# A spectral block with a SwiGLU layer in split fp32r: the first half's layout, layer two's weight parts and output sets, the order of two late steps, and where the planner's sweep begins

## The chip, the cores and the metric

The kernel runs on one core of a Trainium2 chip. The metric is the device time of one execution in microseconds, and the number for a version is the median over several runs. The core has five instruction streams that run side by side and wait for each other through semaphores: TensorE (PE in the profile) multiplies, VectorE (DVE), ScalarE (ACT) and GpSimd (POOL) do elementwise work, SyncE (SP) issues DMAs; ACT and POOL issue some too. Each stream runs its instructions strictly in order.

## The reference

A sequence of 4096 rows with 640 features goes through two residual blocks. Cut to what matters:

```python
x = A_x                                             # (1, 1, 4096, 640)
h = layernorm(x) * (1 + ca) + sa
x = x + ga * A_ref(h)
h = layernorm(x) * (1 + cb) + sb
x = x + gb * ((silu(h @ w_gate) * (h @ w_up)) @ w_down)      # w_gate: 640 x 1728

def A_ref(x):
    z = rfft2(x, axes=(1, 2)).reshape(..., 4, 160)           # H is 1: a DFT over 4096 rows
    hr = relu(zr @ w1[0] - zi @ w1[1] + b1[0])               # per block of 160
    hi = relu(zi @ w1[0] + zr @ w1[1] + b1[1])
    or_ = softshrink(hr @ w2[0] - hi @ w2[1] + b2[0], 0.01)
    oi_ = softshrink(hi @ w2[0] + hr @ w2[1] + b2[1], 0.01)
    return irfft2(or_ + 1j * oi_)
```

The six vectors sa, ca, ga, sb, cb, gb come from `silu(c) @ w_mod`. All data is float32.

## The kernel before, in words

**Split matmuls.** A float32 product is made of three fp32r products. An operand is split into a high part (a copy rounded to fp32r, mostly by ACT) and a low part (the operand minus its high part, mostly by DVE), and PE adds high·high, high·low and low·high in PSUM. So almost everything that PE multiplies has first been through ACT and then DVE, and a late low part is what PE can be seen to wait for.

**First half (to about 310 us), ordered by hand.** The rows come in as tiles `xa0` to `xa7`, are normalised, go through the first DFT step (`dft_a`) and are written to DRAM (`s1`, by `write_s1`) to be read back in another order. Then a loop over p goes through 28 regular slots (p = 0 to LAST; a slot is one block b of 160 features of one chunk ch of frequencies, p = 4 ch + b; there are 8 chunks), and a few tail slots follow. In a slot each engine gets its pieces in the order in which the calls stand:

- `stage_b(ch, t)` is the second DFT step on PE. `evac_b` splits its result into `z` (high on ACT, low on DVE: L603, L604). `evac_rh` and `evac_rl` do the same for the rest features, into `rz` (L626, L636).
- `stage_l1` is layer one (PE L657, L670). Its relu and split make `h` (ACT L660, L661, then DVE L662) and `u` (DVE L675). `tail_l1` and `tail_low` split the rest into `r` (ACT L682, DVE L687).
- `stage_l2(ch, b)` is layer two: for each half q eight matmuls into a PSUM tile `pc` (PE L707), with the weight parts `w2a`, `w2b` and `w2c`; then a DVE addition (L709) writes `pc` plus the bias into the output set `tt` of the chunk. Of a chunk's four blocks the first takes two `tt` tiles (one for each q), of which there are two in all.
- At the next chunk's first block `move_x` moves the finished set by DMA into `xx` tiles. `shrink`, `shrink_high` (ACT, `xh`) and `shrink_low` (DVE L749, `xl`) make the softshrink and its split; `stage_i` is the inverse DFT's first step (PE L760 to L762).

The weights of layer two are split by six jobs (`prep2`): for each of w2a, w2b, w2c two halves of 160 columns, o = 0 and 1. Job 0 is half 0 of w2a, job 1 half 1 of w2a, jobs 2 and 3 those of w2b, 4 and 5 those of w2c. A high part is one instruction (POOL L281 or ACT L283), a low part one on DVE (L286), except that of job 5, which POOL makes with a TENSOR_TENSOR (L523). Before the loop POOL makes the high parts of jobs 0, 2 and 5 and the low part of 5, ACT the high part of job 1, DVE the low parts of 0 and 1. In slot 0, after `stage_l2` has been called for nothing, ACT makes the high parts of 3 and 4 and DVE the low parts of 2, 3 and 4. The first layer-two matmuls stand in slot 1.

The tiles `w2a` to `w2c`, `acc`, `cl`, `wx`, `bx`, `tt` and `xx` are in a pool `p2`, opened once the pool `xp` of the `xa` tiles is closed. Its tiles take over `xp`'s memory, and an instruction that writes a tile there waits for whatever still reads the `xa` tile that had the place, among it the DMAs that write it to `s1`.

**Second half (from about 310 us), ordered by a planner.** A second layer norm and the SwiGLU layer go over six row tiles, the first two in the plain way (`plain`, PE L1951 to L1953), the last four with seven products in place of eight (`seven`, PE L2028 to L2030 and L2039 to L2041). Steps with a planned duration stand in chains: `prep` splits the weights (`wb`: ACT L1413, DVE L1420), `gate` and the others load, add up and split what the coming stages need, and `tails` holds short chains that the matmul stages leave behind: the splitting of activations (`a`, `a13`: ACT L1987, L1925, DVE L1988, L1926) and of the left operands `L` (ACT L2104, DVE L2108). While the planner walks along PE's matmuls it calls `sweep()` every 0.3 planned us; a sweep goes through the chains in a fixed order and issues (`tries`) each next step whose planned start is near enough. What comes first in a sweep takes the engine first.

Of the kernel before, what the change touches and what calls it, by code (L numbers as in the profile page):

```python
# [6 lines left out]
F32 = mybir.dt.float32  # L7
# [11 lines left out]
NB = 4  # L19
# [154 lines left out]
def body(tc, x, w1, b1, w2, b2, wg, wu, wd, c, wm, k_fa, k_tb, k_tx, k_bm, k_bx, k_ga, k_ge, k_id, out, dbg=None):  # L174
# [4 lines left out]
    def f32(ap):  # L179
        return ap.bitcast(F32)  # L180
# [21 lines left out]
    with ExitStack() as top:  # L202
# [35 lines left out]
        with ExitStack() as af:  # L238
# [101 lines left out]
            with tc.tile_pool(name="sp", bufs=1) as sp:  # L340
                xas = []

                def load_x(t):
                    xa = xp.tile([P, 4, D], F32, name=f"xa{t}")
                    if t < 3:
                        for i in range(4):
                            nc.sync.dma_start(xa[:, i, :], xv[:, 4 * t + i, :])
                    else:
                        nc.sync.dma_start(xa, xv[:, 4 * t:4 * t + 4, :])
                    xas.append(xa)  # L350
# [158 lines left out]

            acc = p2.tile([P, D], F32, name="acc")  # L510
# [3 lines left out]
            w2a = p2.tile([P, NB, 640], F32R, name="w2a")  # L514
            w2b = p2.tile([P, NB, 640], F32R, name="w2b")
            w2c = p2.tile([P, NB, 640], F32R, name="w2c")
# [3 lines left out]
            for n in (0, 2, 5):  # L520
                weights_high(*prep2[n], pool)
            w, h, l, v, _ = prep2[5]
            pool.tensor_tensor(w[:, :, l], v, f32(w[:, :, h]), op=OP.subtract)  # L523
# [61 lines left out]
            tts = {}  # L585
# [105 lines left out]
            def stage_l2(ch, b, then=()):  # L691
                h0, h1, r2, _ = hss[ch, b]
                de = slice(160 * b, 160 * b + 160)
                for q in ((0, 2, 1) if ch == CE else (0, 1)):
# [3 lines left out]
                    if b == 0 and q < 2:  # L698
                        tts[ch, q] = p2.tile([P, 2, D], F32, tag="tt", bufs=2, name=f"tt{ch}_{q}")
# [8 lines left out]
                    if q < 2:  # L708
                        dve.tensor_tensor(tts[ch, q][:, :, de], pc[:, :320].rearrange("p (r e) -> p r e", r=2),  # L709
                                          b2t[:, :, b, :], op=OP.add)  # L710
                        if then:
                            then[q]()
                    else:

                        dve.tensor_tensor(tts[ch, 0][0:1, 1, de], pc[0:1, :160], b2t[0:1, 0, b, :], op=OP.add)
# [55 lines left out]
            pool.memset(zero, 0.0)  # L771
            pool.tensor_copy(edge, zero)

# [19 lines left out]
            for job in prep2[0:2]:  # L793
                weights_low(*job)
# [31 lines left out]
            for p in range(LAST + 1):  # L826
# [22 lines left out]
                on(tail_l1, p)  # L849
                on(shrink_high, p - 6)  # L850
                for k in rows:
                    on(evac_rl, k)
                on(tail_low, p)
                on(stage_l2, p - 1)
                if p == 3:
                    stage_b(1, 2)
                    evac_b(1, 2)
                on(stage_i, p - 7)
                on(shrink_low, p - 6)
                if p < LAST:  # L860
                    on(shrink_parts, p - 5)
# [3 lines left out]
                if p == 0:  # L865
                    for n in (3, 4):
                        weights_high(*prep2[n])
                    for job in prep2[2:5]:
                        weights_low(*job)
                if p == 0:  # L870
                    pool.dma_start(bm.rearrange("p a b c -> p (a b c)"), k_bm)
# [173 lines left out]
        with ExitStack() as ff:  # L1045
# [166 lines left out]
            def sweep():  # L1212
                held = NT
                for c in tails + chains:
                    if c in tile_of:
                        if tile_of[c] > held:
                            continue
                        tries(c)
                        if c.steps:
                            held = tile_of[c]  # L1220
                    else:
                        tries(c)
                tails[:] = [c for c in tails if c.steps]
# [1293 lines left out]
```

## Time and profile before

| | us |
|---|---|
| three runs | 1419.41, 1421.2, 1422.27 (median 1421.2) |
| the profiled execution, its own time | 1421.44 |
| its span, first to last instruction | 1419.6 |
| PE busy | 1386.4 (98% of the span) |
| DVE, ACT, POOL busy | 1055.8 (74%), 766.7 (54%), 599.3 (42%) |

Where PE is busy for nearly the whole span, a shorter time can only come from the stretches in which it isn't, or from those in which its clock is lowered. The list of PE's waits names for each matmul line what ended its idle time, and the timeline shows single instructions with the idle time before them in brackets.

### The profile page before, as it was taken

To read this page: it belongs to the slowest core of one execution; us is meant where nothing else is said; L and a number is where in the kernel's file an instruction comes from. 1 tells how busy PE (TensorE), PEld (TensorE's weight loads), DVE (VectorE), ACT (ScalarE), POOL (GpSimd) and SP (SyncE) were. 2 spreads that over 40 slices of the span, in tenths; PEclk is the share of its full clock that TensorE was granted. 3 is DMA by queue.
4 is the path that set the end of the run, shared out by engine and by line. 5 is a ranking of instruction groups with operands and counts; after the bars stand their busy time and mean duration, and the time that the engine had idled before them with its cause. 6 is when DMAs were issued, how large, how long until landed. Compare 5 with 4: busy or idle time off the path is not lost.

```text
span 1419.6 us, 23748 instructions
## 1 busy us (share of the span) xinstructions
PE 1386.4 (98%) x8410; PEld 1311.5 (92%) x8410; DVE 1055.8 (74%) x1863; ACT 766.7 (54%) x1542; POOL 599.3 (42%) x681
## 2 busy tenths in 40 slices
PE   6899999999999999999999999999999999999998
PEld 2599999977989899899999999999999999999998
DVE  8979888889888888649786758787678757365654
ACT  6869999756555545546463446446264624252341
POOL 5600210047767765336454535357153524052241
PEclk9999999999999999999999999999999999999999
DMA  9866556666797997899867998788998667965634
GB/s 360 314 235 201 166 170 193 204 224 205 272 369 283 316 339 267 284 372 320 308 207 274 351 342 287 279 296 270 373 319 289 228 219 274 339 209 194 216 118 148
DMA packets 170872, 377.34 MB, mean 266 GB/s; under 512 B 22177, under 2 KB 81633, under 8 KB 168738
## 3 DMA queue, kind: packets, MB, share of 16 engines
q1 hardware_dynamic: 161650, 359.28, 72.9%
q0 software_dynamic: 6800, 13.93, 3.0%
q10 hardware_dynamic: 2304, 2.62, 0.5%
q8 instruction: 66, 1.08, 0.3%
q14 instruction: 52, 0.43, 0.1%
HBM read 269.48 MB, written 96.80 MB: 258 GB/s over the span
## 4 chain that ended last, share of the span: by engine, by line
PE 83%; DVE 5%; ACT 3%; DMA 3%; POOL 2%; issue 2%; SPq 1%; ACTq 0%; DVEq 0%; POOLq 0%
PE pw L2028 9%; PE pw L2030 9%; PE pw L2029 9%; PE pc L2329 8%; PE pd L2245 7%; PE pe L2329 6%; PE pg L1953 4%; PE pg L1952 4%; PE pg L1951 4%; PE pc L707 4%; PE pl L657 3%; PE pw L2041 2%; PE pw L2039 2%; PE pw L2040 2%; PE py L1666 2%
## 5 line engine op out<-in xcount | busy, mean ns | idle before, releaser
L1420 DVE TENSOR_TENSOR wb<-r,wb 128x768 fp32r<-128x768 f32 (+3 forms) x170 | 161.8, 961 | 11.5 <-ACT wb L1413 11.0
L2028 PE MATMUL pw<-h,wt 128*128 128x384 f32 x412 | 139.4, 338 | 1.7 <-ACT s_v L2047 1.4
L2030 PE MATMUL pw<-h,wt 128*128 128x384 f32 x412 | 138.3, 336 | 0.0
L2029 PE MATMUL pw<-h,wt 128*128 128x384 f32 x412 | 138.0, 335 | 0.0
L2108 DVE TENSOR_TENSOR L<-sg,L 128x384 fp32r<-128x384 f32 x144 | 106.8, 762 | 38.0 <-ACT L L2104 37.3
L1413 ACT ACTIVATE wb<-r 128x768 fp32r<-128x768 f32 (+3 forms) x168 | 104.3, 638 | 53.4 <-PE pw L2041 42.7
L2329 PE MATMUL pc<-wq,L 128*128 128x320 f32 x846 | 132.2, 309 | 0.0
L2329 PEld LDWEIGHTS pc<-wq,L 128*128 128x128 f32 x846 | 126.2, 188 | 0.7 <-DVE s_v L2054 0.3
L2088 POOL TENSOR_TENSOR sg<-s_x,sg 128x384 f32<-128x384 f32 x24 | 31.4, 1307 | 218.3 <-DVE s_x L2054 218.3
L2028 PE MATMUL pw<-h,wb 128*128 128x384 f32 x312 | 105.0, 336 | 0.0
L2029 PE MATMUL pw<-h,wb 128*128 128x384 f32 x312 | 104.4, 335 | 0.0
L2030 PE MATMUL pw<-h,wb 128*128 128x384 f32 x312 | 104.3, 334 | 0.0
L2329 PE MATMUL pe<-wq,L 128*128 128x320 f32 x648 | 102.4, 310 | 1.4 <-DMA wq<-wqd 1.4
L1953 PE MATMUL pg<-ht,wb 128*128 128x512 f32 x260 | 101.4, 390 | 1.5 <-DVE wb L1420 1.5
L1951 PE MATMUL pg<-ht,wb 128*128 128x512 f32 x260 | 101.9, 392 | 0.0
L2047 ACT ACTIVATE s_x<-pw 128x384 f32<-128x384 f32 x52 | 25.5, 491 | 140.9 <-PE pw L2030 138.9
L1952 PE MATMUL pg<-ht,wb 128*128 128x512 f32 x260 | 101.3, 390 | 0.0
L2099 POOL TENSOR_TENSOR sg<-sg,sg 128x384 f32<-128x384 f32 x72 | 92.1, 1279 | 17.2 <-DVE L L2108 13.7
L2329 PEld LDWEIGHTS pe<-wq,L 128*128 128x128 f32 x648 | 96.6, 188 | 1.7 <-DVE x L2286 1.7
L2245 PE MATMUL pd<-wq,a 128*128 128x320 f32 x632 | 96.0, 310 | 0.0
L2245 PEld LDWEIGHTS pd<-wq,a 128*128 128x128 f32 x632 | 93.4, 188 | 0.5
L764 POOL DMA_DIRECT2D s<-co x28 | 15.8, 563 | 180.0 <-ACT co L763 176.7
(317 smaller groups left out, 3903.3 us busy)
## 6 DMA issues: line engine op xcount, KB each, us to landing
wq<-wqd SPq DMA_DIRECT2D x83, 640.0 KB, 5.7
wt<-td SPq DMA_DIRECT2D x103, 512.0 KB, 5.2
hs<-ho SPq DMA_DIRECT2D x52, 512.0 KB, 5.9
h<-hs SPq DMA_DIRECT2D x32, 768.0 KB, 7.9
td<-wt SPq DMA_DIRECT2D x25, 512.0 KB, 5.3
r<-in_B_w_gate_dram SPq DMA_DIRECT2D x24, 384.0 KB, 5.2
r<-in_B_w_up_dram SPq DMA_DIRECT2D x24, 384.0 KB, 4.0
xx<-tt SPq DMA_DIRECT2D x56, 160.0 KB, 3.2
```

The lines of the kernel that those rows point to most:

```text
L1413: def high(ks, e=slice(0, c), copy=lambda o, i: act.activation(o, i, AF.Copy)):
L1420: dve.tensor_tensor(wbs[t, n][:, 1, ks, e], raw[t, n][:, ks, e], f32(wbs[t, n][:, 0, ks, e]), op=OP.subtract)
L1951: mm(b, wh, hh, start=(kk == 0), stop=False)
L1952: mm(b, wh, hl, start=False, stop=False)
L1953: mm(b, wl, hh, start=False, stop=(kk == 4))
L2028: mm(b, w(0, kp), a[:, kp, 0], start=start and kp == 0, stop=False, skip_group_check=not start)
L2029: mm(b, w(0, kp), a[:, kp, 1], start=False, stop=False, skip_group_check=not start)
L2030: mm(b, w(1, kp), a[:, kp, 0], start=False, stop=kp == 1, skip_group_check=not start)
L2099: pool.tensor_tensor(o, x, y, op=op)
L2108: dve.tensor_tensor(o[:, 1], raws[j], f32(o[:, 0]), op=OP.subtract)
L2245: mm(b[:, :320], l, m, start=start and i == 0, stop=stop and i == len(s) - 1)
L2329: mm(o[:, :320], ls[q][:, x, k], w[:, q, y], start=start and q == 0 and n == 0, stop=q == 1 and n == 2, skip_group_check=not start)
```

## The change

The first half, the diff cut to its core:

```diff
                 xas = []
+                xts = {t: xp.tile([P, 4, D], F32, name=f"xa{t}") for t in (1, 2, 3, 0, 4, 5, 6, 7)}
 
                 def load_x(t):
-                    xa = xp.tile([P, 4, D], F32, name=f"xa{t}")
+                    xa = xts[t]
...
+            w2a = p2.tile([P, NB, 640], F32R, name="w2a")
+            w2b = p2.tile([P, NB, 640], F32R, name="w2b")
+            w2c = p2.tile([P, NB, 640], F32R, name="w2c")
             acc = p2.tile([P, D], F32, name="acc")
             cl = p2.tile([P, D], F32, name="cl")
             wx = p2.tile([P, P], F32, name="wx")
             bx = p2.tile([P, 2, 128], F32, name="bx")
-            w2a = p2.tile([P, NB, 640], F32R, name="w2a")
-            w2b = p2.tile([P, NB, 640], F32R, name="w2b")
-            w2c = p2.tile([P, NB, 640], F32R, name="w2c")
+            p2.tile([P, 896], F32, name="gap")
+            tts = {(1, q): p2.tile([P, 2, D], F32, tag="tu", bufs=2, name=f"tt1_{q}") for q in range(2)}
             prep2 = prep_weights(raws[2], w2a, w2b, w2c, False)
 
             prep2 = [prep2[i] for i in (0, 3, 1, 4, 2, 5)]
-            for n in (0, 2, 5):
+            for n in (0, 2):
                 weights_high(*prep2[n], pool)
-            w, h, l, v, _ = prep2[5]
-            pool.tensor_tensor(w[:, :, l], v, f32(w[:, :, h]), op=OP.subtract)
+
+            def weights_rest(n):
+                w, h, l, v, _ = prep2[n]
+                pool.tensor_tensor(w[:, :, l], v, f32(w[:, :, h]), op=OP.subtract)
...
-            def stage_l2(ch, b, then=()):
+            def stage_l2(ch, b, then=(), held=None):
...
-                    if b == 0 and q < 2:
-                        tts[ch, q] = p2.tile([P, 2, D], F32, tag="tt", bufs=2, name=f"tt{ch}_{q}")
+                    if b == 0 and q < 2 and ch != 1:
+                        tts[ch, q] = p2.tile([P, 2, D], F32, tag="tu" if ch % 2 else "tt", bufs=2, name=f"tt{ch}_{q}")
...
-                        dve.tensor_tensor(tts[ch, q][:, :, de], pc[:, :320].rearrange("p (r e) -> p r e", r=2),
-                                          b2t[:, :, b, :], op=OP.add)
+                        add = lambda q=q, pc=pc: dve.tensor_tensor(
+                            tts[ch, q][:, :, de], pc[:, :320].rearrange("p (r e) -> p r e", r=2), b2t[:, :, b, :], op=OP.add)
+                        if held is None:
+                            add()
+                        else:
+                            held.append(add)
...
             weights_high(*prep2[1])
-            for job in prep2[0:2]:
-                weights_low(*job)
+            weights_low(*prep2[0])
+            weights_rest(1)
+            weights_high(*prep2[3], pool)
+            weights_rest(3)
...
-                on(tail_l1, p)
-                on(shrink_high, p - 6)
+                for f in (shrink_high, tail_l1) if p == LAST else (tail_l1, shrink_high):
+                    on(f, p if f == tail_l1 else p - 6)
                 for k in rows:
                     on(evac_rl, k)
-                on(tail_low, p)
-                on(stage_l2, p - 1)
+                if p == LAST:
+                    on(shrink_low, p - 6)
                 if p == 3:
+                    adds = []
+                    stage_l2(0, 2, held=adds)
                     stage_b(1, 2)
                     evac_b(1, 2)
+                    on(tail_low, p)
+                    for f in adds:
+                        f()
+                else:
+                    on(tail_low, p)
+                    on(stage_l2, p - 1)
                 on(stage_i, p - 7)
-                on(shrink_low, p - 6)
                 if p < LAST:
+                    on(shrink_low, p - 6)
                     on(shrink_parts, p - 5)
...
                 if p == 0:
-                    for n in (3, 4):
+                    for n in (4, 5):
                         weights_high(*prep2[n])
-                    for job in prep2[2:5]:
-                        weights_low(*job)
-                if p == 0:
+                    weights_rest(5)
+                    for n in (2, 4):
+                        weights_low(*prep2[n])
+                    pool.memset(zero, 0.0)
+                    pool.tensor_copy(edge, zero)
                     pool.dma_start(bm.rearrange("p a b c -> p (a b c)"), k_bm)
```

The second half:

```diff
             def sweep():
                 held = NT
-                for c in tails + chains:
+                for c in [gate, prep] + tails + chains:
```

What it does, part by part. (a) **Layout:** the `xa` tiles get their places in the order 1, 2, 3, 0, 4 to 7, and the weight tiles come first in `p2`. Before, `w2a`, `w2b`, `w2c` and `tt` had the places of `xa1`, `xa2`, `xa3` and `xa4`; now `w2a` lies in memory that no `xa` tile had, `w2b` on `xa1`, `w2c` on `xa2`, `acc` to `bx` on `xa3`, the new set `tu` on `xa0`, and `tt` still on `xa4`. (b) **Weight parts:** POOL makes the high parts of jobs 0, 2 and 3 and the low parts of 1, 3 and 5, ACT the high parts of 1, 4 and 5, DVE the low parts of 0, 2 and 4 only. (c) **Output sets:** chunks with an odd number write to a second set, `tu`. (d) **Slot 3:** the two additions of `stage_l2(0, 2)` are held back until `evac_b(1, 2)` and `tail_low` are issued. (e) **Slot LAST:** ACT makes `xh` ahead of the rest's relu, and DVE makes `xl` ahead of `tail_low` and of layer two's additions. (f) **Sweep:** `gate` and `prep` are tried ahead of `tails`, and again in their old place.

How the instructions moved is shown at three places. The first is POOL's stream in the first half, from layer two's first weight part on (`rm` and `rr` are the raw weights; L281 makes high parts; `bm` is the inverse DFT's matrix). Before:

```order
L281 TENSOR_SCALAR w2a<-rm_596 128x4x160
L281 TENSOR_SCALAR w2b<-rm_596 128x4x160
L281 TENSOR_SCALAR w2c<-rr_597 128x4x160
L523 TENSOR_TENSOR w2c<-rr_597,w2c 128x4x160
L771 MEMSET zero 128x40
L772 CAST edge<-zero 128x40
L871 DMA bm<-in_k_bm_dram 128x512
```

and now:

```order
L281 TENSOR_SCALAR w2a<-rm_596 128x4x160
L281 TENSOR_SCALAR w2b<-rm_596 128x4x160
L528 TENSOR_TENSOR w2a<-rm_596,w2a 128x4x160
L281 TENSOR_SCALAR w2b<-rm_596 128x4x160
L528 TENSOR_TENSOR w2b<-rm_596,w2b 128x4x160
L528 TENSOR_TENSOR w2c<-rr_597,w2c 128x4x160
L886 MEMSET zero 128x40
L887 CAST edge<-zero 128x40
L888 DMA bm<-in_k_bm_dram 128x512
```

POOL has two subtractions more, and `zero`, `edge` and the load of `bm` come behind them.

The second is DVE's stream in row tile 1, about 483 us into the span, where `wb1_3` is the weight group 3 of that tile, `wq` and `tq` are parts of the down weights, `a1_1_1_1` and `a13_1` low parts of activations, `x9` a residual row. Before:

```order
L1420 TENSOR_TENSOR wb1_3_5794<-r1_3_5388,wb1_3_5794 128x512
L1532 TENSOR_TENSOR wq1_1_1_5801<-wdr1_1_5683,wq1_1_1_5801 128x2x320
L1988 TENSOR_TENSOR a1_1_1_1_5788<-sg1_0_1_5724,a1_1_1_0_5787 128x512
L1920 TENSOR_TENSOR sgr1_5822<-pg1_2_0_5790,sgr1_5822 64x512
L1420 TENSOR_TENSOR wb1_3_5794<-r1_3_5388,wb1_3_5794 128x768
L1573 TENSOR_TENSOR tq0_1_5818<-wdr1_0_5345,tq0_1_5818 128x2x320
L1926 TENSOR_TENSOR a13_1_5821<-sgr1_5822,a13_1_5821 64x512
```

and now:

```order
L1437 TENSOR_TENSOR wb1_3_5801<-r1_3_5397,wb1_3_5801 128x512
L2005 TENSOR_TENSOR a1_1_0_1_5766<-sg1_0_0_5700,a1_1_0_0_5765 128x512
L1687 TENSOR_TENSOR x9_5577<-x9_5577,py9_0_5815 128x320
L1437 TENSOR_TENSOR wb1_3_5801<-r1_3_5397,wb1_3_5801 128x768
L2005 TENSOR_TENSOR a1_1_1_1_5795<-sg1_0_1_5727,a1_1_1_0_5794 128x512
L1937 TENSOR_TENSOR sgr1_5839<-pg1_2_0_5797,sgr1_5839 64x512
L1549 TENSOR_TENSOR wq1_1_1_5804<-wdr1_1_5698,wq1_1_1_5804 128x2x320
```

The second low part of the weight group stood behind three other instructions since the first, and now stands behind two with fewer elements; `wq`, the second `a` part and `sgr` come after it.

The third is ACT's stream at the start of row tile 2's weight group 3, about 643 us into the span (`s2_3_x`, `s2_3_v`, `s2_3_y` copy PSUM results, `a13_2_1` is an activation's high part, `ho3` the next tile's rows). Before:

```order
L2047 ACTIVATE s2_3_x_7507<-pw2_3_0_7496 128x384
L2104 ACTIVATE L05_7165<-sg2_0_10_7279 128x384
L1925 ACTIVATE a13_2_1_7492<-sgr2_1_7493 64x384
L2104 ACTIVATE L06_7166<-sg2_0_00_7274 128x384
L1766 ACTIVATE ho3_0_1_7533<-h32_3_0_7315 128x2x128 x2
L2047 ACTIVATE s2_3_v_7539<-pw2_3_3_7528 128x384
```

and now:

```order
L2064 ACTIVATE s2_3_x_7503<-pw2_3_0_7492 128x384
L1430 ACTIVATE wb2_4_7500<-r2_4_7349 128x768
L2121 ACTIVATE L05_7179<-sg2_0_10_7257 128x384
L2121 ACTIVATE L06_7180<-sg2_0_00_7252 128x384
L2064 ACTIVATE s2_3_v_7548<-pw2_3_3_7537 128x384
L1783 ACTIVATE ho3_0_0_7553<-h32_3_0_7389 128x2x128 x2
```

`s2_3_v` now stands ahead of `ho3` and of `a13_2_1`, and the weight group's larger high part ahead of `L05`.

More of the change, by code (lines that the diff above doesn't have):

```diff
@@ L584, in body @@
             hss = {}
-            tts = {}
             def width(ch):
@@ L770, in body @@
             zero = hp.tile([P, 2, 5, 2, 2], F32, name="zero")
-            pool.memset(zero, 0.0)
-            pool.tensor_copy(edge, zero)
             def edges():
```

## The prediction

> **What bounds the kernel now.** I read the page first, then the list of PE's waits, then windows, then the timeline around each long wait.
>
> ```profile
> span 1419.6 us, 23748 instructions
> PE 1386.4 (98%) x8410; PEld 1311.5 (92%) x8410; DVE 1055.8 (74%) x1863; ACT 766.7 (54%) x1542; POOL 599.3 (42%) x681
> ```
>
> PE is the bound: it idles 1419.6 − 1386.4 = 33.2 us in all, and no matmul is added or removed here. So a gain can come only from those 33.2 us and from stretches of lowered clock. The waits, by what ended them (total, times, longest):
>
> ```profile
> PE pa L437 <- ACT xa L416: 9.8, 2, 8.0
> PE pc L707 <- DVE w2b L286: 2.4, 1, 2.4
> PE py L1666 <- DVE chl L1656: 1.9, 1, 1.9
> PE pg L1953 <- DVE wb L1420: 1.5, 1, 1.5
> PE pb L596 <- DVE z L604: 1.5, 2, 1.0
> PE pi L761 <- DVE xl L749: 1.0, 1, 1.0
> PE pi L760 <- DVE u L675: 1.0, 2, 0.8
> ```
>
> The largest, 9.8, is the start, before anything that the change moves. The `chl` wait stays too: it lies between the halves, ahead of the place (about 410 us) from which the second half's order differs. What remains is a handful of waits of 1 to 2.4 us. I go through them by the parts of the change.
>
> **Slot 3, additions held back (d).**
>
> ```profile
> 88.24 0.89 DVE L709 TENSOR_TENSOR tt<-pc,b2t 128x320 f32<-128x320 f32 x2
> 89.05 0.74 DVE L604 SCALAR_TENSOR_TENSOR z<-pb,ca,z 128x512 fp32r<-128x512 f32 x1
> 89.85 1.16 PE L596 MATMUL pb<-tb,g 128*128 128x128 f32 x8 [1.03 <-DVE z L604]
> 90.76 0.69 PE L707 MATMUL pc<-w2a,h 128*128 128x320 f32 x3
> ```
>
> PE waits 1.03 us for the PSUM bank that this `z` frees, and `z` stands behind the two additions (0.89) and the `r` before them. With the additions held back `z` starts about 1.2 us earlier, ahead of the `r` too, and `stage_b` follows the matmul before it. The additions come about 0.75 later (`z`'s 0.74); they free PSUM tiles that the next layer-two group takes only from 90.76, after the end of the delayed additions at about 89.9, so they are covered. Were that cover gone, PE would lose up to 0.75. **−1.0.**
>
> **Slot LAST (e).**
>
> ```profile
> 265.95 0.72 ACT L744 ACTIVATE xh<-xx 128x640 fp32r<-128x640 f32 x1
> 267.12 0.89 DVE L709 TENSOR_TENSOR tt<-pc,b2t 128x320 f32<-128x320 f32 x2
> 267.92 0.81 DVE L749 TENSOR_TENSOR xl<-xx,xh 128x640 fp32r<-128x640 f32 x1
> 268.79 0.41 PE L761 MATMUL pi<-xl,bm 128*128 128x320 f32 x1 [1.05 <-DVE xl L749]
> ```
>
> `xl` needs only `xh`, finished at 266.67, or 266.3 with `xh` ahead of the relu. Ahead of `r` and the additions it runs at 266.7 instead of 267.9, 1.2 earlier, and the wait of 1.05 goes. The additions move 0.8 later; the next layer-two group, which needs their PSUM tiles, stands behind the rest of `stage_i` and the whole of the next layer one, over 2 us. Without that cover up to 0.8 would come back. **−1.0.**
>
> **Two output sets (c).** In the stretch from 60 to 300 us DVE's waits have this row, and the one that reaches PE is the second:
>
> ```profile
> DVE tt L709 <- DMA xx<-tt: 9.5, 6, 2.2
> 129.53 0.49 DVE L709 TENSOR_TENSOR tt<-pc,b2t 128x320 f32<-128x320 f32 x1 [1.84 <-DMA xx<-tt]
> 133.69 0.41 PE L760 MATMUL pi<-xh,bm 128*128 128x320 f32 x1 [0.80 <-DVE u L675]
> ```
>
> At six chunk boundaries the first addition waits for the DMA that moves the last set out, 9.5 us of DVE time; with a second set the buffer's last reader is a whole chunk further back. Only part reaches PE: from 129.53 on DVE is busy without a gap up to the `u` that ends at 133.6, and PE waits 0.80 for it; a second wait on `u` (the list has 1.0 for both) has the same cause. **−1.0.** The other boundaries' waits ended before PE had run out of work, no row of PE's list goes back to them, and they are worth nothing.
>
> **Weight parts and layout (a, b).** This is the first half's largest wait.
>
> ```profile
> 69.12 0.41 PE L707 MATMUL pc<-w2b,h 128*128 128x320 f32 x1 [2.41 <-DVE w2b L286]
> 70.01 0.39 PE L707 MATMUL pc<-w2c,r 128*128 128x320 f32 x1 [0.33 <-DVE w2c L286]
> 72.00:73.00 1.00, 1.00 (x6) 1.00 (x6) 0.96 (x3) 0.00 (x0) 0.00 (x0) 0.50 1.07 370
> 74.00:75.00 1.00, 1.00 (x9) 1.00 (x8) 0.67 (x2) 0.58 (x2) 0.00 (x0) 0.79 1.04 389
> 60.85 1.56 DVE L286 SCALAR_TENSOR_TENSOR w2a<-rm,w2a 128x640 fp32r<-128x640 f32 x2
> 66.26 2.81 DVE L286 SCALAR_TENSOR_TENSOR w2b<-rm,w2b 128x640 fp32r<-128x640 f32 x2
> 68.99 0.87 DVE L286 SCALAR_TENSOR_TENSOR w2c<-rr,sgn,w2c 128x640 fp32r<-128x640 f32 x1
> 61.67 2.41 POOL L281 TENSOR_SCALAR w2b<-rm 128x640 fp32r<-128x640 f32 x1 [3.06 <-DMA s<-xa]
> 56.70 1.91 POOL L281 TENSOR_SCALAR w2a<-rm 128x640 fp32r<-128x640 f32 x1 [4.82 <-PE pb L596]
> 59.84 0.74 ACT L283 ACTIVATE w2a<-rm 128x640 fp32r<-128x640 f32 x1
> 66.06 1.57 POOL L523 TENSOR_TENSOR w2c<-rr,w2c 128x640 fp32r<-128x640 f32 x1
> ```
>
> PE waits 2.41 + 0.33 = 2.74 us, and after it the granted clock (the last but two of a window's numbers) is 0.50 from 71 to 74 and 0.79 from 74 to 75. That is about 3.4 us at half clock, or 1.7 us of matmuls lost. So this place costs 4.4 in all. What releases PE is DVE at 69.07 and 69.87. DVE's rows have no idle time in brackets there, so it must get less to do or do it faster: it loses two low parts (0.78 each, by the `w2a` row). Against that, the 2.81 for two `w2b` parts shows 1.25 beyond twice 0.78, and the first of them began 0.2 after POOL's subtraction, which ran from 66.06 to 67.6. POOL now makes three such subtractions in place of one, the first as soon as `w2a`'s high half is there (60.6).
>
> So I replay it. `w2b`'s high part no longer waits 3.06 for a DMA: its place was `xa2`'s, now `xa1`'s, written out earlier, so it runs at 58.7. The first subtraction runs from 60.6 to 62.2. **If POOL and DVE exclude each other**, DVE's `w2a` low part starts at 62.2 instead of 60.85 and ends at 63.0, and `h`, `u`, `z`, `rz` and `r` end at about 66.9 instead of 66.2. POOL's last subtraction (from 66.05) holds `w2b`'s low part until 67.6, so the two low parts end at about 68.5 and 69.3, against 69.07 and 69.87. That gains 0.5, less about 0.2 to 0.5 because the earlier `stage_b` (the 0.5 beside the 1.0 in the list's `z` row) waits longer for a later `z`. **If they don't**, they end at about 66.9 and 67.8, POOL's last part decides at 67.7, and the wait shrinks by 1.5 to 2.2; then the clock may stay up, 1.7 more. The bounds are +0.5 and −3.9. The 2.81 is this very pair of operations, so I lean on it: **−0.3**. ACT makes two high parts in slot 0 as before, and what is queued behind POOL's added 3 us is `zero`, `edge` and the load of `bm`, which nobody needs for several slots.
>
> The Trainium skill ("SBUF — State Buffer", Who interferes with whom) states the rule that speaks against this part: a DVE instruction with two SBUF inputs contends with a GpSimd instruction that reads SBUF, and it describes the shared port pair as an exclusive lock. The trace agrees as far as the 2.81 goes; by the rule the term is the −0.3, without it it would be near −3.9.
>
> On the clock, "TensorE: Matmul & The Clock Gate" (table in Why this matters for your kernels) asks for no idle gaps above about 3 us. By it a wait of 2.74 would cost no clock, and this part could win 2.2 at most; the 0.50 rows say otherwise here, and the measurement decides.
>
> **The sweep (f).** It changes where steps stand, not how many there are. From 410 us on:
>
> ```profile
> 410.00:1419.00 1009.00, 999.15 (x5985) 972.84 (x5983) 700.61 (x1185) 454.76 (x936) 453.50 (x461) 1.00 0.80 277
> 483.82 1.36 DVE L1532 TENSOR_TENSOR wq<-wdr,wq 128x640 fp32r<-128x640 f32 x1
> 485.11 1.22 DVE L1988 TENSOR_TENSOR a<-sg,a 128x512 fp32r<-128x512 f32 x1
> 486.98 0.94 DVE L1420 TENSOR_TENSOR wb<-r,wb 128x768 fp32r<-128x768 f32 x1
> 487.98 0.50 PE L1953 MATMUL pg<-ht,wb 128*128 128x512 f32 x1 [1.52 <-DVE wb L1420]
> 646.96 0.71 ACT L1766 ACTIVATE ho<-h 128x256 fp32r<-128x256 f32 x2
> 648.09 0.45 PE L2028 MATMUL pw<-h,wt 128*128 128x384 f32 x1 [1.09 <-ACT s_v L2047]
> ```
>
> PE idles 1009 − 999.15 = 9.9 us there, the most that the sweep can win. Two of its waits lie where the order shows a remedy. The `wb` wait of 1.52: the low part now stands ahead of `wq`, the second `a` part and `sgr`, which took from 483.8 to 487.0; two additions and subtractions with fewer elements are put there instead, so it is some 2 us earlier. The `s_v` wait of 1.09: `s_v` is put ahead of `ho` (0.71) and `a13_2_1`. That is −2.6. The other 7.3 us are drawn anew; I put them at the same amount, and allow +1.0 for new waits where activations' splits now give way. **−1.6**, between −5 and +4.
>
> **The sum.** −1.0 − 1.0 − 1.0 − 0.3 − 1.6 = −4.9. The profiled execution took 1421.44 (its span of 1419.6 and 1.8 around it), so 1416.5; it lies 0.2 above the median of 1421.2, so 1416.3 against that: **1416**.
>
> **The rivals.**
>
> *The weight wait and the clock drop go too.* Then −3.9 stands in place of −0.3: 1416 − 3.6 = **1412.4**. For it: DVE is freed of two parts, and a wait a little shorter may escape the clock drop, as the 1.9 of `chl`, which lies in this window, did (clock 1.00):
>
> ```profile
> 325.00:350.00 25.00, 23.10 (x106) 19.13 (x105) 24.38 (x32) 13.60 (x21) 16.79 (x13) 1.00 0.74 238
> ```
>
> Against it: the 2.81. 20%.
>
> *The gain does not show.* The planner gives back what the first half wins, or the held instructions open waits of their own: 1421.2 − 3.3 of the first half + 2.5 lost behind it, **1420.4**, within 0.2% (2.8 us, about what a measurement of this kernel can tell from no change). For it: 7.3 us of waits are redrawn blind. Against it: the first half's four waits each have one named cause which the edit takes away. 19%.
>
> *Slower: weight parts ahead of the left operands.* With `prep` tried before `tails`, DVE may take a weight low part just before the first `L` low part that a down stage is waiting for. The price is one such part:
>
> ```profile
> L1420 DVE TENSOR_TENSOR wb<-r,wb 128x768 fp32r<-128x768 f32 x77 | 93.9, 1219 | 4.8 <-ACT wb L1413 4.6
> ```
>
> Four row tiles of three down stages make 12 × 1.22 = 14.6 if every one is hit and none has slack: 1421.2 − 3.3 + 14.6 = **1432.5**; half of them gives 1425. It decides from 6.1 us, five hits, on (1424.0). Against it: no wait in PE's list was ended by an `L` or `a` step (L2108, L2104, L1988), so there was slack, and DVE is busy only 700.61 of 1009 there. 11%.
>
> **How the numbers follow.** The forecast has 50%, the rivals 20, 19 and 11. Faster by over 0.2% (below 1418.4) are the forecast and the first rival, 0.70; same 0.19; slower (above 1424.0) 0.11. The forecast's own range is 1413 to 1418.4. To leave out no more than 2 in 10 it reaches down past the first rival's 1412.4 and up over the third's 1420.4: **1410 to 1421.5**.
>
> **What would show it.** Right: no PE wait at the `stage_b` near 89 us nor at `xl` near 267; no DVE row of `tt` waiting for `xx<-tt`; `w2b`'s high part on POOL beginning near 58.7; DVE's first `w2a` low part lasting over 1.5 us, and PE still waiting over 2 us near 67, with a window at 0.50 behind it. Wrong: that wait below 1 us and no window under 1.00 (then 1412); PE idle from 410 us on above 12 us (then 1420 and more); or PE waits ended by L2125 or L2121, the new lines of the `L` parts (the slower rival).

## The result, and the profile after

In the first measurement the changed kernel took 1416.01 us (median of 6 executions, 1415.61 to 1417.25) and the kernel before 1422.68 (6 executions, 1419.41 to 1427.03): a ratio of 0.9954, 95% interval 0.9937 to 0.9970. Measured twice more among the experiments it came to 0.9969 (0.9955 to 0.9983) and 0.9940 (0.9924 to 0.9957). So it is faster: by 0.2 to 0.8% over the three intervals, and by 4.4 to 8.5 us by the three ratios. The forecast, 1416 against 1421.2, was 5.2 us. The forecast holds as a sum; not all of its terms do.

The page of the changed kernel's profiled execution (1417.25 us) begins so:

```profile
span 1415.5 us, 23753 instructions
PE 1385.5 (98%) x8410; PEld 1313.2 (93%) x8410; DVE 1071.2 (76%) x1861; ACT 764.0 (54%) x1542; POOL 601.1 (42%) x683
```

PE's idle time fell from 33.2 to 30.0 us. The start (10.2) and `chl` (1.9) are about as they were; these further rows of the list of PE's waits (total, times, longest) bear on the change:

```profile
PE py L1683 <- DMA gt<-in_k_ga_dram: 1.9, 2, 1.6
PE pc L711 <- POOL w2b L528: 1.6, 1, 1.6
PE pc L711 <- POOL w2c L528: 1.5, 1, 1.5
PE pw L2056 <- ACT s_z L2064: 1.4, 1, 1.4
PE pi L768 <- DVE u L679: 1.2, 2, 1.0
PE pi L768 <- ACT cz L822: 0.6, 1, 0.6
PE pw L2045 <- ACT s_y L2064: 0.6, 1, 0.6
PE pi L821 <- ACT co L771: 0.5, 1, 0.5
```

Gone are the waits on `z` (1.0 near 89 us), `xl` (1.0 near 267), `wb` (1.5) and `s_v` (1.1). The wait on `u` is still there, and layer two's weights hold PE for 1.6 + 1.5 us and another 0.2, 3.3 in place of 2.7, now ended by POOL. New are a wait for a DMA (`gt`, a matrix of the last inverse DFT step in the second half, whose load POOL issues), `s_z`, `s_y`, and some tenths in the tail slots (`cz`, `co`).

### The profile page after: what moved, and what is told of

Read it like the earlier page. It is cut to its first block, busy times and chain, and to the rows that moved or that the text cites. A ratio compares the mean times of both kernels' runs of the same rounds, so it can differ in the third digit from the quotient of the medians.

```text
span 1415.5 us, 23753 instructions
## 1 busy us (share of the span) xinstructions
PE 1385.5 (98%) x8410; PEld 1313.2 (93%) x8410; DVE 1071.2 (76%) x1861; ACT 764.0 (54%) x1542; POOL 601.1 (42%) x683
## 5 line engine op out<-in xcount | busy, mean ns | idle before, releaser
L1437 DVE TENSOR_TENSOR wb<-r,wb 128x768 fp32r<-128x768 f32 (+3 forms) x170 | 175.6, 1043 | 12.5 <-ACT wb L1430 12.3
L2125 DVE TENSOR_TENSOR L<-sg,L 128x384 fp32r<-128x384 f32 x144 | 100.8, 724 | 26.5 <-ACT L L2121 26.0
```

Source lines behind the costliest of these rows:

```text
L1437: dve.tensor_tensor(wbs[t, n][:, 1, ks, e], raw[t, n][:, ks, e], f32(wbs[t, n][:, 0, ks, e]), op=OP.subtract)
L2125: dve.tensor_tensor(o[:, 1], raws[j], f32(o[:, 0]), op=OP.subtract)
```

## The experiments

All were timed in jobs with the kernel before on the same chip. The granted clock is the mean over the executions.

| run | what it is | median us | ratio to before (95%) | clock |
|---|---|---|---|---|
| e1_sweep | before, new sweep | 1422.25 | 1.0008 (0.9997 to 1.0019) | 0.9971 |
| e2_nosweep | changed, old sweep | 1420.67 | 0.9994 (0.9977 to 1.0011) | 0.9976 |
| e3_slots | before, slots 3 and LAST | 1423.21 | 1.0005 (0.9991 to 1.0020) | 0.9980 |
| e4_parts | changed, weight parts as before | 1417.18 | 0.9975 (0.9964 to 0.9987) | 0.9981 |
| e5_again | changed | 1418.73 | 0.9969 (0.9955 to 0.9983) | 0.9974 |
| e6_two_wm | changed, two `wm` buffers | 1422.56 | 1.0010 (0.9997 to 1.0023) | 0.9965 |
| e7_fresh | changed, other places and parts | 1416.90 | 0.9960 (0.9947 to 0.9973) | 0.9972 |
| e8_step | before, sweeps every 0.28 | 1433.76 | 1.0072 (1.0057 to 1.0088) | 0.9960 |
| e9_places | changed, new places, parts as before | 1414.87 | 0.9935 (0.9918 to 0.9952) | 0.9985 |
| e10_early_wm | e9, `wm` loads earlier | 1412.39 | 0.9920 (0.9900 to 0.9940) | 0.9985 |
| e11_nosweep | changed, old sweep | 1421.39 | 0.9992 (0.9977 to 1.0007) | 0.9968 |
| e12_after | changed | 1415.33 | 0.9940 (0.9924 to 0.9957) | 0.9983 |

e1 to e4 ran in one job (before: median 1421.72), e5 to e8 in a second (1421.98), e9 to e12 in a third (1423.47).

### The sweep alone, and everything but the sweep (e1, e2, e11, e12)

e1 is the kernel before with this; e2 and e11 are the changed kernel without it:

```diff
-                for c in tails + chains:
+                for c in [gate, prep] + tails + chains:
```

> The kernel before with only the sweep changed. Theory (the sweep's gain is its own): PE's idle time from 410 us on falls from 10.3 to about 8.4 us as in the changed kernel, the waits of 1.52 (wb) and 1.09 (s_v) are gone, and the time is 2 to 3 us below the kernel before. Rival (what came off in the second half hangs on the first half's timing): idle time there stays at 10 us and the time within 1 us of before.

> The changed kernel with the old sweep. Theory: it keeps what the first half won, the two waits at about 89 and 267 us (1.0 each), and loses the sweep's part: 1.5 to 2.5 us below before, 2 to 3 above the changed kernel, with the waits on wb and s_v back. Rival (layout, weight parts and sets carry the gain): 4 us or more below before.

Alone neither half can be told from no change. e1 is as its rival said. For e2 the interval leaves out the rival's 4 us (it ends at 3.3 below) but not the theory's 1.5 to 2.5. That did not fit the whole, so the changed kernel was measured again (e5), and in the third job beside its version without the sweep:

> The changed kernel once more, beside the kernel before on another day's chip, since single executions of either spread over 8 us and the parts run alone (the sweep, or all but the sweep) showed no gain. Theory (the whole gains more than its parts because its worst executions, with several stretches of half clock, are fewer): a ratio of 0.995 to 0.998, a median 3 to 6 us below before. Rival (the first measurement was lucky in its executions): a ratio above 0.998.

> The changed kernel with the old sweep once more, beside the changed kernel on the same chip. Theory (on top of the new first half the sweep's new order is worth 2 to 3 us): 1.5 to 3.5 us above the changed kernel in this job. Rival (the sweep is worth nothing, as it was alone): within 1 us of it.

> The changed kernel, as the measure for the three runs beside it: 3 to 5 us below before.

e5 lies 3.3 us below before by its median, as its theory said; e12 lies 8.1 below, more than expected. In that job the sweep is worth 1421.39 − 1415.33 = 6.1 us on top of the new first half, more than the theory's 2 to 3. The size rests on this one job: the interval of e5 (0.9955 to 0.9983) overlaps those of e2 and e11. Windows from 410 us on, for e1, e11 and e12, in this order (first the stretch, then PE's busy time):

```profile
410.00:1425.00 1015.00, 999.42 (x5993) 974.55 (x5992) 714.21 (x1190) 455.02 (x937) 454.57 (x459) 1.00 0.80 276
```
```profile
410.00:1425.00 1015.00, 998.14 (x5966) 971.49 (x5964) 700.03 (x1181) 453.75 (x934) 449.63 (x456) 1.00 0.79 275
```
```profile
410.00:1425.00 1015.00, 995.25 (x5965) 970.43 (x5964) 709.34 (x1182) 453.13 (x935) 450.39 (x455) 1.00 0.79 274
```

With the spans (1419.2, 1418.6, 1414.0 us) PE's idle time from 410 us on is 1419.2 − 410 − 999.42 = 9.8, then 10.5, then 8.8 us; before it was 10.5. The other profiles show how far this varies by itself: the changed kernel has 8.5 (first measurement) and 9.1 (e5), e2 has 10.9, and e3, with the old sweep on the old first half, 9.5. So on the new first half the sweep saves 1.3 to 2.3 us of idle time, and on the old one no saving can be told (9.8 against 10.5 and 9.5). e11 shows what else it saves. Its longest wait of the second half, and a window behind it (clock third from the right):

```profile
PE pw L2056 <- ACT s_z L2064: 2.3, 1, 2.3
653.00:654.00 1.00, 1.00 (x5) 1.00 (x4) 1.00 (x3) 0.21 (x2) 0.00 (x0) 0.50 0.80 299
```

After this wait of 2.3 us the clock is halved for 3.4 us, 1.7 us of matmuls. Idle time and clock make 3.4 of the 4.6 us between these two executions, and e11's mean clock of 0.9968 against 0.9983 is 2.1 us of 1420. The rest of the 6.1 stays open.

The same wait of 2.3 us and the same stretch of half clock stand in e2's profile, and the kernel before has neither. This is one reason why the new first half alone shows no gain: from 85 to 310 us PE idles only 2.6 us in e2 and 2.8 in e11, against 4.3 before, but behind that both lose more at `s_z` than the kernel before lost at `s_v` (1.1). The sweep's new order has a price as well. PE waits for `gt` near 512 us in all nine profiles with the new order (1.5 to 4.1 us) and in none of the five with another. In e1, where the waits on `wb` and `s_v` are gone, it is the second row of PE's list:

```profile
PE py L1666 <- DMA gt<-in_k_ga_dram: 1.9, 1, 1.9
```

With 1.4 on `s_z` and 1.3 on `s_y`, new or longer there, it takes the place of what e1 saved.

### Another order without a meaning (e8)

```diff
-                    d = min(n, 0.3)
+                    d = min(n, 0.28)
```

> The kernel before with the planner's sweeps every 0.28 instead of 0.3 planned us, a change with no meaning for priorities that draws the second half's order anew. Theory (what the sweep change did to the second half is a redraw): PE's idle time from 410 us on moves by 1 to 3 us either way, as much as with the sweep change. Rival (the priority of the weight parts is what counts): idle time there stays within 0.5 us of 10.3.

Idle time from 410 us on went to 1433.7 − 410 − 1005.94 = 17.8 us, seven us worse and more than the theory's 1 to 3, by several waits of which these are the largest (the list of PE's waits and one window):

```profile
PE pw L2030 <- DVE wb L1420: 3.8, 3, 1.9
PE pt L1729 <- ACT xn L1697: 3.1, 2, 2.2
PE pw L2028 <- ACT s_y L2047: 2.7, 1, 2.7
410.00:1433.70 1023.70, 1005.94 (x5990) 977.68 (x5988) 715.10 (x1187) 454.04 (x937) 449.16 (x460) 0.99 0.79 273
```

A change to the planner that says nothing of priorities moves the time by 12 us, three more stretches of half clock included. So a planner change is a redraw first, and the idle time that the sweep saves is no proof that its priority is the better one.

### The two slots alone (e3)

The diff is parts (d) and (e) of the change, put into the kernel before.

> The kernel before with only slot 3's held additions and slot LAST's new order. Theory: PE's waits on z near 89 us and on xl near 267 us are gone, nothing else in the first half changes, and the time is 2.0 us below before. Rival (the additions, now later, hold up layer two's PSUM tiles): new PE waits of 0.5 us or more behind them and a time within 1 us of before.

Both waits went: of `z` only the earlier one of 0.5 near 63 us is left, and the 0.5 on `xl` is another, at 283 us. But PE waits more in the tail slots, `co` 1.2 in place of 0.3. PE's waits in e3, and one in e1, whose slots are those of before:

```profile
PE pi L818 <- ACT co L767: 1.2, 1, 1.2
PE pb L596 <- DVE z L604: 0.5, 1, 0.5
PE pi L765 <- DVE xl L753: 0.5, 1, 0.5
```
```profile
PE pi L814 <- ACT co L763: 0.8, 1, 0.8
```

The waits show −2.0 and +1.4. e1's 0.8 says that `co` varies without the edit, so it is not shown that the held instructions caused the +1.4. The timing excludes a gain above 1.3 us (0.9991), so the theory fell as to time, though not as to the waits, and the rival's place was wrong too: what came up stands some 20 us later in the tail, not at layer two's PSUM tiles. Where the saved waits went in time stays open for this run.

### Layer two's weights (e4, e7)

In the changed kernel DVE, POOL and PE look like this (timeline), with a window behind:

```profile
66.08 2.16 DVE L286 SCALAR_TENSOR_TENSOR w2c<-rr,sgn,w2c 128x640 fp32r<-128x640 f32 x1
68.16 2.10 DVE L666 TENSOR_TENSOR h<-h,h 128x256 fp32r<-128x256 f32 x2
65.50 2.05 POOL L528 TENSOR_TENSOR w2b<-rm,w2b 128x640 fp32r<-128x640 f32 x1
67.51 2.11 POOL L528 TENSOR_TENSOR w2c<-rr,w2c 128x640 fp32r<-128x640 f32 x1
67.61 0.42 PE L711 MATMUL pc<-w2b,h 128*128 128x320 f32 x1 [1.58 <-POOL w2b L528]
69.68 0.42 PE L711 MATMUL pc<-w2c,r 128*128 128x320 f32 x1 [1.51 <-POOL w2c L528]
72.00:73.00 1.00, 1.00 (x7) 1.00 (x7) 0.86 (x2) 0.00 (x0) 0.00 (x0) 0.50 1.04 371
```

DVE's `w2c` part takes 2.16 us beside POOL's subtraction (0.87 before the change), and the pair `h` takes 2.10 beside the next (0.75 before). e4 keeps the changed layout and has POOL make only what it made before:

```diff
-            for n in (0, 2):
+            for n in (0, 2, 5):
                 weights_high(*prep2[n], pool)
+            weights_rest(5)
...
-            weights_low(*prep2[0])
-            weights_rest(1)
-            weights_high(*prep2[3], pool)
-            weights_rest(3)
+            for job in prep2[0:2]:
+                weights_low(*job)
...
-                    for n in (4, 5):
+                    for n in (3, 4):
                         weights_high(*prep2[n])
-                    weights_rest(5)
-                    for n in (2, 4):
-                        weights_low(*prep2[n])
+                    for job in prep2[2:5]:
+                        weights_low(*job)
```

> The changed kernel's layout, but the weight parts made as before (POOL the high parts of jobs 0, 2, 5 and the low part of 5; ACT 1, 3, 4; DVE the low parts of 0 to 4). In the changed kernel POOL releases PE, by six operations in a row from 58.3 to 69.6 us, and PE waits 3.25 us. Theory (POOL's chain is what is late): here POOL is done by about 65.5 us, DVE's low parts end at about 67.3 and 68.1, PE waits 1.9 us in all, and the time is 1.3 us below the changed kernel, 3 below if the clock then stays up. Rival (POOL and DVE exclude each other, whoever makes the parts): the wait stays at 2.7 us or more and the time equals the changed kernel's within 0.5 us.

```profile
63.44 1.55 POOL L528 TENSOR_TENSOR w2c<-rr,w2c 128x640 fp32r<-128x640 f32 x1
65.55 1.56 DVE L286 SCALAR_TENSOR_TENSOR w2b<-rm,w2b 128x640 fp32r<-128x640 f32 x2
74.99 0.89 DVE L714 TENSOR_TENSOR tt<-pc,b2t 128x320 f32<-128x320 f32 x2 [3.79 <-DMA s<-xa]
67.16 0.42 PE L712 MATMUL pc<-w2b,h 128*128 128x320 f32 x1 [1.17 <-DVE w2b L286]
75.54 0.71 PE L712 MATMUL pc<-w2a,h 128*128 128x320 f32 x3 [1.66 <-DVE tt L714]
72.00:73.00 1.00, 1.00 (x11) 1.00 (x11) 0.00 (x0) 0.82 (x3) 0.00 (x0) 1.00 1.06 406
```

Since the place of `w2b` is free earlier, POOL's subtraction is over before DVE starts on `w2b`, and the same two parts take 1.56 us in place of 2.81. The weight wait falls to 1.17 + 0.33, and the clock stays up. But the next thing is late: the first additions wait 3.79 us for the DMAs that write `xa4` out, whose place `tt` has, and PE loses 1.66 to them. In the changed kernel that wait was hidden behind the longer one (1.4 us on DVE, none on PE). So the theory's shorter wait came and its time did not: e4's ratio is no lower than the changed kernel's three. The rival's 2.7 us or more is excluded.

e7 gave the first output set the memory that no `xa` tile had, put w2a, w2b, w2c on `xa1` to `xa3`, and let ACT make w2b's high parts:

> The changed kernel with the first chunk's output set in the memory that no xa tile had, w2a, w2b, w2c on xa1, xa2, xa3, and the weight parts made by POOL (high parts of jobs 0 and 5, low part of 5, all before DVE's low parts of w2b begin), ACT (high parts of 1, 2, 3, 4) and DVE (low parts of 0 to 4). Theory: POOL's subtraction ends before 65.5 us, DVE's low parts take 0.8 us each, PE waits 1.5 to 2.0 us at layer two's first group instead of 3.25, and the wait of 1.66 on the first output additions near 74 us, seen with the weight parts made as before, does not appear: 1 to 1.5 us below the changed kernel, 3 below where the clock stays up. Rival (w2b's high part, behind the write of xa2, is late again): a wait of 2.5 us or more.

```profile
65.43 2.10 POOL L529 TENSOR_TENSOR w2c<-rr,w2c 128x640 fp32r<-128x640 f32 x1
65.31 2.90 DVE L286 SCALAR_TENSOR_TENSOR w2b<-rm,w2b 128x640 fp32r<-128x640 f32 x2
```

The additions no longer wait, but `w2c`'s place is `xa3`'s, and POOL's high part there begins only at 63.53 and its subtraction at 65.43, beside DVE's two parts again: 2.90 us for them, and a wait of 2.1 on PE with the clock halved behind it. The wait lies between the theory's 2.0 and the rival's 2.5, and came by way of `w2c`, not of `w2b`. The median is 1.8 us below e5's, with intervals that overlap. Three kernels with the two operations side by side (2.81, 2.90, and 2.16 for one part) and three without (1.56 in e4, e9 and e10) settle it: the collision is real.

### The wait on u, and the modulation rows (e6, e10), and the places (e9)

With two output sets DVE no longer waits for the last set's DMAs. It waits for something else (the changed kernel):

```profile
129.65 0.89 DVE L543 SCALAR_TENSOR_TENSOR acc<-wm,sc,acc 128x640 f32<-128x640 f32 x1 [2.10 <-DMA wm<-in_w_mod_dram]
132.64 0.42 PE L768 MATMUL pi<-xh,bm 128*128 128x320 f32 x1 [1.01 <-DVE u L679]
```

`acc` stands between the addition and `u` on DVE. e6 gave the row two buffers, taking the memory from the unused tile `gap`:

```diff
-            p2.tile([P, 896], F32, name="gap")
+            p2.tile([P, 256], F32, name="gap")
...
-                wmts[m, k] = p2.tile([P, D], F32, tag="wm", bufs=1, name=f"wm{m}_{k}")
+                wmts[m, k] = p2.tile([P, D], F32, tag="wm", bufs=2, name=f"wm{m}_{k}")
```

> The changed kernel with two buffers for the modulation rows (wm) instead of one, so that a row's DMA need not wait for the addition of the row before. Theory (with two output sets the wait near 131 us stayed because DVE's acc addition now waits 2.1 us for such a DMA): that DVE wait is gone or below 0.5 us, PE's wait on u (1.0 us) goes with it, and the time is 1 us below the changed kernel. Rival (u is late for another reason, ACT's or DVE's own order): PE still waits 0.8 us or more for u there.

DVE's waits from 60 to 300 us, and one of PE's:

```profile
DVE tt L713 <- DMA s<-xa: 7.0, 1, 7.0
DVE acc L543 <- DMA wm<-in_w_mod_dram: 7.0, 4, 2.4
PE pc L711 <- DVE tt L713: 4.9, 1, 4.9
```

The waits for `wm` stayed, and PE's on `u` with them (1.3): a second buffer was not what the DMA lacked. And the smaller `gap` moved the tiles behind it by 2560 bytes a partition. DVE then waits 7.0 us for the write-out of an `xa` tile before it may write `tt`, where the changed kernel has 1.4; that `tt` now also touches the place of a tile written out later is inferred from this. It costs 4.9 us of PE, and the run is 4 us over the changed kernel. So the run says little of `wm`'s worth, and a lot of what `gap` is for.

e9 therefore placed everything by when its memory comes free (w2a unused memory, w2b `xa1`, w2c `xa2`, the first set `xa3`, `acc` to `bx` `xa4`, the second set `xa0`), with the weight parts of e4 and the load of `bx` later; e10 adds the second `wm` buffer and issues its loads ahead of the moves:

```diff
-                xts = {t: xp.tile([P, 4, D], F32, name=f"xa{t}") for t in (1, 2, 3, 0, 4, 5, 6, 7)}
+                xts = {t: xp.tile([P, 4, D], F32, name=f"xa{t}") for t in (1, 2, 3, 4, 0, 5, 6, 7)}
...
             w2c = p2.tile([P, NB, 640], F32R, name="w2c")
+            tts = {(0, q): p2.tile([P, 2, D], F32, tag="tt", bufs=2, name=f"tt0_{q}") for q in range(2)}
             acc = p2.tile([P, D], F32, name="acc")
...
+                early = [x for x in mods.get(p, ()) if x[0] is mod_load]
+                for f, *a in early:
+                    f(*a)
                 if b == 0 and ch:
                     for i in range(4):
                         move_x(ch - 1, i)
```

> The changed kernel with w2a in the memory that no xa tile had, w2b on xa1, w2c on xa2, the first chunk's output set on xa3, acc to bx on xa4, the second set on xa0, the load of bx moved behind slot 3's loads, and the weight parts made as before the change. Theory (made as before, POOL's subtraction is over before DVE reaches w2b, and what then held PE was the output set on xa4's place): PE waits about 1.5 us at layer two's first group in place of 3.3, DVE's two w2b parts take 1.6 us and not 2.8, no wait of 1 us or more on the first additions near 74 us; a median 2 to 3.5 us below the changed kernel in the same job, the clock at 1.00 between 66 and 76 us. Rival (the place only hands the wait on): another wait of 1.5 us or more appears before 80 us and the time is the changed kernel's within 1 us.

> The kernel with the new places, and in addition two buffers for the modulation rows, whose DMAs are issued ahead of the DMAs that move an output set in the same slot. Theory (the row's DMA lands late because it is issued behind those moves): DVE's waits of 2 us for wm near 130 us go, PE's wait of about 1 us for u near 131 us goes, 1 us less than with the new places alone. Rival (DMAs are late for their traffic, not for their order): the waits stay, the time equals that with the new places alone.

The additions to `acc` in e9 and in e10, and for each the first layer-two wait and a window behind it, e9 first:

```profile
126.79 0.89 DVE L544 SCALAR_TENSOR_TENSOR acc<-wm,sc,acc 128x640 f32<-128x640 f32 x1 [2.00 <-DMA wm<-in_w_mod_dram]
67.19 0.42 PE L712 MATMUL pc<-w2b,h 128*128 128x320 f32 x1 [1.15 <-DVE w2b L286]
72.00:73.00 1.00, 0.77 (x8) 0.67 (x7) 0.99 (x4) 0.85 (x3) 0.00 (x0) 1.00 1.02 393
```
```profile
125.63 0.88 DVE L544 SCALAR_TENSOR_TENSOR acc<-wm,sc,acc 128x640 f32<-128x640 f32 x1
67.61 0.41 PE L712 MATMUL pc<-w2b,h 128*128 128x320 f32 x1 [1.25 <-DVE w2b L286]
71.00:72.00 1.00, 1.00 (x7) 1.00 (x6) 0.94 (x3) 0.00 (x0) 0.00 (x0) 0.50 1.03 407
```

In e9 the weight wait is 1.15 + 0.33, no wait above 0.3 follows before 80 us, and the clock stays up. In e10 the wait for `wm` and PE's wait on `u` are gone. But its weight wait, 1.25 + 0.33 us, is followed by half clock all the same, so the shorter wait alone does not keep the clock up; this profiled execution is the slowest of e10's six (1416.8). In time e9 is only 0.5 us below the changed kernel of its job, less than the theory's 2 to 3.5 and not to be told from nothing; its profiled execution shows one reason, a `gt` DMA that PE waits 3.8 us for at 507 us, with two stretches of half clock behind it:

```profile
PE py L1683 <- DMA gt<-in_k_ga_dram: 3.8, 1, 3.8
```

e10 is 2.5 us below e9, where the theory said 1; executions of each spread over 5 to 7 us, so the time of this step is not settled. With a median of 1412.39 e10 lies 2.9 below the changed kernel and 11.1 below the kernel before in the same job. The ratios to before of e10 (0.9900 to 0.9940) and of the changed kernel (0.9924 to 0.9957) overlap, so that it beats the changed kernel is likely but not settled; that it beats the kernel before is.

## Why the prediction was right, point by point

- **Slot 3 (−1.0).** The wait on `z` near 89 us went in the changed kernel and in e3, and stayed where the edit was absent (e1 has it in its list as 1.0). Right.
- **Slot LAST (−1.0).** The wait on `xl` near 267 us went. But the tail slots wait more behind it: `co` and `cz` took 0.5 + 0.6 + 0.2 us in the changed kernel's first profile (0.5 in the other two) against 0.5 before, and in e3 1.2 with a new 0.5 on `xl`. The cover held for layer two, as predicted. Whether the edit makes ACT's copies in the tail late is not shown, since e1 has 0.8 on `co` without it. Between a little and nearly all of the term is left.
- **Two output sets (−1.0).** This term failed. The step at fault is "a second wait on `u` has the same cause": DVE's wait for `xx<-tt` went as predicted, but two places behind it in the same stream the addition to `acc` needs a DMA (`wm`) that lands just as late, and `u` stayed late by 1.0 to 1.3 us in all three profiles. I had followed one releaser and not asked which DMA is next. In e10's profile the wait is gone once that load is issued earlier.
- **Weight parts and layout (−0.3).** Right in mechanism: POOL and DVE held each other, the gain of the shorter lists was eaten, and the half clock came each time. PE waited 3.3, 2.9 and 2.0 us in the three profiled executions of the changed kernel, with 0, 0.8 and 0.9 more for the earlier `z`, against 2.7 and 0.5 before. So the term came out between +0.5 and −0.3, nothing that stands out of the spread. In e12 POOL began at 56.6, as the replay assumed (56.7), and the replay's end comes out to a tenth: POOL's last subtraction at 66.06 (66.05), and DVE's first `w2b` part, held by it, to 68.4 (68.5).

```profile
66.06 1.66 POOL L528 TENSOR_TENSOR w2c<-rr,w2c 128x640 fp32r<-128x640 f32 x1 [0.28 <-PE pb L600]
66.34 2.06 DVE L286 SCALAR_TENSOR_TENSOR w2b<-rm,w2b 128x640 fp32r<-128x640 f32 x1
```

In the first profile the raw weights landed later, POOL began at 58.3, and its last parts, not DVE's, ended the waits at 67.6 and 69.6. The sign "DVE's first `w2a` low part lasting over 1.5 us" came in e12 alone (2.03; 1.04 and 0.82 in the others).
- **The sweep (−1.6).** The wait on `wb` went for the reason given: it is 1.6 in e2 and e11, where the sweep is the old one. The wait on `s_v` went too, but it falls to 0.3 in e2 and e11 as well, so that is not the sweep's doing alone. Idle time from 410 us on fell by 1.9 us in the first profile (10.5, where the prediction counted 9.9 up to 1419.0, to 8.5). As a term for the time it was mis-sized: on top of the new first half it was worth 6.1 us in the one job that compares them, of which the profiles account for 3.4, a longer wait on `s_z` and a clock drop behind it; on the old first half no gain showed. I costed it against the kernel before, where the `s_z` wait does not stand, and the wait for `gt` that its order brings was not foreseen beyond the allowance of 1.0.
- **The rivals.** The first rival, weight wait and clock drop gone, needed the parts made otherwise and other places (e4, e9). The second, that the gain does not show, describes each half alone and not the whole. The slower rival, `L` or `a` parts late behind weight parts, did not come: no wait of PE in the changed kernel was ended by them.

That the sum was met at 1416 is therefore partly luck: −1.0 for the output sets, the −0.3 and part of slot LAST did not come, and the sweep gave more.

## What to carry to other kernels

Where a stream waits for a late buffer, look at the next instructions behind it in that stream and at what each of them needs, before crediting the wait that is removed; here another DMA, landing at the same time, stood two instructions behind. A tile's place in reused memory is a dependence like any other: sort the tiles by when the old owners' DMAs end, and give the first needed the first free. In e9 this shortened the waits; that it shortened the time is not shown. And measure a planner's change together with what runs ahead of it: here no gain showed alone, and six us in the one job that had it on top of the other edits.

## What the runs showed of the hardware

**The clock falls after waits well under 3 us, and not every time.** In the changed kernel's profile a wait of 1.94 us on `chl` at 327 us was followed by 3.4 us at half clock; the same wait in the kernel before (1.9) was not. Before in the first fence, the changed kernel in the second, each with the wait and a window some 2 us behind it:

```profile
331.09 0.41 PE L1666 MATMUL py<-chl,gt 128*128 128x320 f32 x1 [1.90 <-DVE chl L1656]
332.00:333.00 1.00, 1.00 (x6) 0.82 (x5) 1.00 (x3) 0.93 (x2) 0.00 (x0) 1.00 1.06 383
```
```profile
328.86 0.41 PE L1683 MATMUL py<-chl,gt 128*128 128x320 f32 x1 [1.94 <-DVE chl L1673]
331.00:332.00 1.00, 1.00 (x4) 0.80 (x3) 1.00 (x2) 0.00 (x0) 0.00 (x0) 0.50 1.13 388
```

e3 had 2.5 + 0.3 us at layer two's weights and no drop behind it, e10 only 1.25 + 0.33 there and a drop. Each drop seen cost 1.7 us of matmuls, or twice that. So between 1.2 and 2.8 us the length of a wait does not tell by itself whether a drop follows; the four waits of 3.7 us and more behind the start (e6, e7, e9, e10) each had one, of the longer kind. The Trainium skill's "TensorE: Matmul & The Clock Gate" (table in Why this matters for your kernels) puts the bound at about 3 us of idle time; single waits well below it were enough here.

**Much of the spread between executions of one kernel goes with this clock.** e9's executions at a granted clock of 1.000 took 1412.85 to 1413.16 us, those at 0.997 took 1416.58 to 1417.69: 0.003 of 1415 us is 4.2. It is not all of it: e5's three executions at 0.998 took 1415.31 to 1419.26. That a kernel with fewer waits of 1 to 2 us gains twice, by the waits and by the drops that then don't come, is likely from this but was not tested.

**A low part on DVE and a subtraction on POOL exclude each other**, by all durations seen: 2.16 us for a part that takes 0.78 alone, where POOL's took 2.05 in place of 1.55. The Trainium skill's "SBUF — State Buffer" (Who interferes with whom) says that a DVE instruction with two SBUF inputs contends with a GpSimd instruction that reads SBUF. The runs agree, with these durations.
